# Numerators of batches 1 to 3 split at the halves of the tokens (288 and 256 columns) instead of 512 and 32

## The chip, the cores and the metric

The kernel runs on one core of one Trainium2 chip. The metric is the device time of one execution in microseconds. Before the change three runs took 291.69, 292.36 and 292.44 us: a median of 292.36 us.

The engines are named as in the profile: PE is TensorE (matmuls; PEld is its loading of weights), DVE is VectorE, ACT is ScalarE, POOL is GpSimd, SP is SyncE, which issues DMAs. Matmuls write to PSUM; DVE and ACT read PSUM and write SBUF.

## The reference

Two blocks, all in float32, with 4 batches, 4 heads, 1088 tokens in each, and head width 32.

```python
def phi(x):
    a = np.einsum('rd,bhsd->bhsr', S1, x)          # r = 8
    b = np.einsum('rd,bhsd->bhsr', S2, x)
    return np.einsum('bhsi,bhsj->bhsij', a, b).reshape(*x.shape[:-1], r * r)
q_p, k_p = (phi(q), phi(k))
kv = np.einsum('bhsf,bhsd->bhfd', k_p, v)
z = np.sum(k_p, axis=2)
num = np.einsum('bhsf,bhfd->bhsd', q_p, kv)
den = np.einsum('bhsf,bhf->bhs', q_p, z)[..., None] + 1e-06
attn = num / den
x = attn.transpose(0, 2, 1, 3).reshape(4352, 128)
gate = 1.0 / (1.0 + np.exp(-(x @ w_gate)))         # w_gate, w_val: 128 x 1536
return (gate * (x @ w_val)) @ w_out                # w_out: 1536 x 128
```

The change concerns `num`, the numerators, and their division by `den`.

## The kernel before, in words

**The second block sets the rhythm.** The tokens are cut into chunks of 512. For each chunk, twelve "waves" (function `w1`, matmuls of line 544) compute 128 columns each of both products with `w_gate` and `w_val` into a PSUM tile `wave` of two banks. There are two such buffers (pool `psm`). ACT takes the sigmoid (`sg`, line 552), DVE multiplies (`g`, function `glu` inside `w1`, line 587), POOL forms sums and differences of `g` (`tsum`, line 371), and further matmuls (`prod`, line 381) multiply by `w_out`. A wave may be written again only when DVE has read the wave that lay in its buffer.

**The first block is woven in between.** The order of the instructions on PE, DVE, ACT and POOL is written out by hand: each engine runs them in the order in which the code issues them. The function `slot(group, n)` issues a `group` of work of the first block and then `n` waves. Batch 0 is done at the start by functions of its own; batches 1 to 3 go through `begin`, `outer`, `sum_z`, `kv_all`, `ndt`, `qmult`, and last `parts`, at fixed places between the waves. So `parts` is called three times. The waves that read a batch's tokens come after its `parts`.

**The tokens of a batch stand in two halves.** `q_chk = [(0, 8), (8, 9)]` cuts the 34 rows of 32 tokens into pairs: 8 pairs and 9 pairs. Half 0 has 8 x 32 = 256 columns for each of two values of `c` (the two members of a pair), half 1 has 9 x 32 = 288 (`W1`). `QP[b]` holds the features `q_p` of both halves, and `half(t, n)` cuts half `n` out.

**What `parts(b)` does before** (lines 1267 to 1299):

1. `den_j` (line 1024): eight matmuls of 160 columns into the tile `denj` of the pool `ps2`, tag `two`, which has one buffer of two banks. Then DVE multiplies these 160 columns of each bank by `A8` into `PD` (line 1037). In the text this product is called `pd`.
2. `glu()`: DVE's product for the last wave.
3. Eight numerator matmuls (`numerators`, line 1259; one for each head and each `c`, 64 rows by 32 columns of the array, so that all eight run beside each other) with 512 columns: 256 of half 0 and the first 256 of half 1. They write a `wave` buffer, called `nps`.
4. ACT copies them to SBUF (`num`, line 1274, 128 x 1024), which lets the wave buffer go.
5. Eight numerator matmuls with the last 32 columns of half 1, in a new tile of tag `two` (`nps2`, in the profile also `nps`), columns 160 to 191. It is the buffer of `denj`, so the matmuls wait for `pd`.
6. `den_i` (line 1040): two matmuls of 160 columns that finish the denominators, in columns 0 to 159 of the same tile.
7. `turn_den` (line 1051): DVE transposes the denominators, adds 1e-6 and takes the reciprocal.
8. For each half: DVE spreads the reciprocals (`rb`, line 1282) and multiplies the numerators by them into `xT` (line 1293): 8 pairs of half 0 from `num`, 8 pairs of half 1 from `num`, and the ninth pair of half 1 from `nps2`.

After `parts`, `slot` issues the `prod` matmuls that are due and the next wave.

Of the kernel before, what the change touches and what calls it, by code (L numbers as in the profile page):

```python
# [8 lines left out]
F32 = mybir.dt.float32  # L9
# [5 lines left out]
MUL = ALU.mult  # L15

P = 128
# [3 lines left out]
def kernel(  # L21
# [12 lines left out]
    nc = tc.nc  # L34

    B, H, S, D = q.shape
# [24 lines left out]
    psm = ctx.enter_context(tc.tile_pool(name="psm", bufs=2, space=bass.MemoryType.PSUM))  # L61
    pso = ctx.enter_context(tc.tile_pool(name="pso", bufs=1, space=bass.MemoryType.PSUM))
    ps2 = ctx.enter_context(tc.tile_pool(name="ps2", bufs=1, space=bass.MemoryType.PSUM))
# [11 lines left out]
    q_chk = [(0, 8), (8, TP - 8)]  # L75
    T0 = 2 * q_chk[0][1]
    W1 = 32 * q_chk[1][1]
# [142 lines left out]
    def step(name, *parts, **how):  # L220
        for n in parts if wide else ():
            if n not in short:

                i = ((slice(0, 2), 0), (slice(0, 2), 1), (2, slice(0, 2)))[n] if n < 3 else (slice(0, 3), n - 1)
                pair, jj = (0, i[1]) if n < 3 else divmod(n - 1, 2)
                short[n] = Short(w_sb[:, i[0], i[1]], w_in[pair][:, i[0], jj])
            getattr(short[n], name)(**how)
# [92 lines left out]
    for c in range(2):  # L320
        rows = slice(64 * c, 64 * c + 64)
        nc.vector.tensor_reduce(
            out=m_col[rows, c],
            in_=ident[rows].rearrange("p (k j) -> p j k", j=R),
            axis=mybir.AxisListType.X,
            op=ALU.add,
        )
    for t, x in (
# [5 lines left out]
        out=e_sum,  # L334
        in_=bass.AP(
            tensor=e_row.tensor,
            offset=e_row.offset,
            ap=[list(e_row.ap[0]), [0, 2], [1, R], [0, R]],
        ),
# [3 lines left out]
    two = const.tile([P, 1], F32, tag="two_", name="two_")  # L343
# [5 lines left out]
    xT = const.tile([P, NTOK], F32, tag="xT")  # L349
# [258 lines left out]
    def glu():  # L608
        if moe["gate"] is not None:
            moe["gate"]()  # L610
            moe["gate"] = None
# [54 lines left out]
    KP, QP, BQ, ND, KAB, ASB, KVZ, KVD, Z4, ZS, A8, B8, ZW, PD, RC = ({} for _ in range(15))  # L666

    WD = 160
# [100 lines left out]
    def half(t, n):  # L769
        return t.rearrange("p (n h w) -> p n h w", n=2, h=H)[:, n, :, : 32 * q_chk[n][1]]  # L770
# [253 lines left out]
    def den_j(b):  # L1024
        t = ps2.tile([P, 2, 512], F32, tag="two", name="denj")
        for pi in range(2):
            rows = slice(64 * pi, 64 * pi + 64)
            for x in range(4):
                nc.tensor.matmul(  # L1029
                    out=t[32 * x : 32 * x + 32, pi, :WD],  # L1030
                    lhsT=ZW[b][rows, 4 * (x % 2) : 4 * (x % 2) + 4].rearrange("p x i -> p (x i)"),
                    rhs=B8[b][rows, (W1 - WD) * (x // 2) : (W1 - WD) * (x // 2) + WD],
                    start=True,
                    stop=True,
                )
        PD[b] = sbA.tile([P, 2, WD], F32, tag="pd", name="pd", bufs=1)
        nc.vector.tensor_tensor(out=PD[b], in0=t[:, :, :WD], in1=A8[b], op=MUL)


    def den_i(b, dps):  # L1040
        for pi in range(2):
            nc.tensor.matmul(  # L1042
                out=dps[64 * pi : 64 * pi + 64],
                lhsT=mask["head"].rearrange("p m x -> p (m x)"),
                rhs=PD[b][:, pi, :],
                start=True,
                stop=True,
            )
        return dps

    def turn_den(b, dps):
        nt, over = WD // 32, (W1 - WD) // 32
        dT = sbA.tile([P, nt, 32], F32, tag="dTi", name="dTi", bufs=1)
        nc.vector.transpose(out=dT.rearrange("p t c -> p (t c)"), in_=dps)
        RC[b] = sbA.tile([P, 2, W1 // 32, 2], F32, tag="rci", name="rci")
        for t0, t1, u0, k in ((0, nt, 0, 0), (nt, W1 // 32, nt - over, 4)):
            nc.vector.tensor_scalar_add(
                RC[b][:, :, t0:t1],
                dT[:, u0 : u0 + t1 - t0, k : k + 4].rearrange("p t (n c) -> p n t c", n=2),
                1e-6,  # L1060
            )
        nc.vector.reciprocal(out=RC[b], in_=RC[b])


    def dn(b, n, mid=None):
# [32 lines left out]


        def divide(*parts, between=None, later=False):  # L1100
            if mid is None:
                turn()
# [39 lines left out]
    else:  # L1142
        nc.vector.tensor_copy(
            out=s4[:, 1:],
            in_=bass.AP(
                tensor=s4.tensor, offset=s4.offset, ap=[list(s4.ap[0]), [0, 3], [1, D]]
            ),
# [5 lines left out]
        out=st_[:, : 2 * R],  # L1153
        lhsT=s4.rearrange("p g d -> p (g d)"),
        rhs=ident[: 2 * R, : 2 * R],
# [8 lines left out]
        out=sk,  # L1164
        in0=bass.AP(
            tensor=st_.tensor, offset=st_.offset, ap=[list(st_.ap[0]), [0, 2], [R, 2], [1, R]]
        ),
        in1=bass.AP(
            tensor=hm.tensor, offset=hm.offset, ap=[list(hm.ap[0]), [R, 2], [0, 2], [1, R]]
        ),  # L1170
        op=MUL,
# [6 lines left out]
    for n, inner in enumerate(([[1, R], [0, R]], [[0, R], [1, R]])):  # L1178
        t = const.tile([P, R, R], F32, tag=f"s{n}", name=f"s{n}")
        s0 = st_[:, n]  # L1180
        nc.scalar.copy(
            out=t, in_=bass.AP(tensor=s0.tensor, offset=s0.offset, ap=[list(s0.ap[0])] + inner)
# [68 lines left out]
        glu()  # L1251
        late.append(dn(0, 1)(later=True))

    def numerators(b, t, rest):
        for h in range(H):
            for c in range(2):
                rows = slice(64 * c, 64 * c + 64)
                q1 = QP[b].rearrange("p (n h w) -> p n h w", n=2, h=H)[rows, :, 2 * (h % 2) + h // 2]
                nc.tensor.matmul(  # L1259
                    out=t[32 * h : 32 * h + 32, c],  # L1260
                    lhsT=ND[b][rows, 32 * h : 32 * h + 32],
                    rhs=q1[:, 1, W1 - 32 :] if rest else q1[:, :, : W1 - 32],
                    start=True,
                    stop=True,
                )

    def parts(b):
        den_j(b)
        glu()
        t = psm.tile([P, 2, 512], F32, tag="wave", name="nps")  # L1270
        numerators(b, t, False)
        num = sbA.tile([P, 2, NJK, 2, F], F32, tag="kp", name="num", bufs=1)
        num = num.rearrange("p c j m f -> p (c j m f)")[:, :1024].rearrange("p (c w) -> p c w", c=2)
        nc.scalar.copy(out=num, in_=t)
        t = ps2.tile([P, 2, 512], F32, tag="two", name="nps2")
        numerators(b, t[:, :, WD : WD + 32], True)
        turn_den(b, den_i(b, t[:, 0, :WD]))
        for n in range(2):
            rb = sbA.tile([P, 9, 2, 32], F32, tag="rb", name="rb")
            t0, tn = q_chk[n]  # L1280
            r0 = RC[b][:, n]
            nc.vector.transpose(
                out=rb[:, :tn].rearrange("p t c s -> p (t c s)"),
                in_=bass.AP(
                    tensor=r0.tensor,
                    offset=r0.offset,
                    ap=[list(r0.ap[0]), [1, 2 * tn], [0, 32]],
                ),
            )
            for u0, u1, x in ((0, 8, num[:, :, 256 * n : 256 * n + 256]), (8, tn, t[:, :, WD : WD + 32])):  # L1290
                if u0 < u1:
                    o = b * S + 64 * (t0 + u0)
                    nc.vector.tensor_tensor(
                        out=xT[:, o : o + 64 * (u1 - u0)].rearrange("p (t c s) -> p c t s", c=2, s=32),
                        in0=x.rearrange("p c (t s) -> p c t s", s=32),
                        in1=rb[:, u0:u1].rearrange("p t c s -> p c t s"),
                        op=MUL,
                    )
        moe["ready"] = b * S + S

    def kv_all(b):
# [31 lines left out]
    load_kq(2)  # L1333
    slot(None, 1)
    slot(lambda: parts(1), 1)
    moe["store"]()

# [64 lines left out]
```

## Time and profile before

| what | value |
|---|---|
| three runs, median | 291.69, 292.44, 292.36; 292.36 us |
| the profiled execution | 291.03 us, of it the span from the first to the last instruction 289.2 us |
| granted TensorE clock, mean | 1.000 |
| numerators, 512 columns: 48 records, median | 589 ns |
| numerators, 32 columns: 48 records, median | 201 ns |
| pd, 128x320: 3, median | 492 ns |
| copy num, 128x1024: 3, median | 1012 ns |
| products from num, 128x512: 6, median | 693 ns |
| product from nps, 128x64: 3, median | 218 ns |

A matmul of float32 leaves two records in the trace, two passes over its columns. Records of matmuls that stand in different parts of the array overlap, and the length of a record includes the way through the array; so the time that a group of matmuls occupies the array is read from the distance of starts, not from the lengths. All times in the views are microseconds from the span's start, if not marked otherwise.

### The profile page before, as it was taken

The page shows a single profiled execution, that of the slowest core. Times are in us where ns is not written, and L with a number is a line of the kernel's source. Part 1 is how long each engine was busy: PE and PEld are TensorE (multiplying, and loading weights), DVE is VectorE, ACT ScalarE, POOL GpSimd, SP SyncE. Part 2 cuts the span into 40 slices and gives each one's busy share as a digit, 9 for nine tenths or more (in the row PEclk, how much of TensorE's full clock was granted, in tenths as well). Part 3 has the DMA queues.
Part 4 walks back from the last instruction along what each step waited for, and adds up shares of the span by engine and source line. Part 5 has one row for each costly group of instructions (what it writes and reads, how often), then busy time and mean ns, then how long its engine had stood idle before and what let it go on. Part 6 is the DMA issues. An engine that isn't in the chain of part 4 may idle for free.

```text
span 289.2 us, 5782 instructions
## 1 busy us (share of the span) xinstructions
PE 282.5 (98%) x2260; PEld 151.2 (52%) x2260; DVE 170.2 (59%) x294; ACT 106.5 (37%) x215; POOL 159.6 (55%) x222
## 2 busy tenths in 40 slices
PE   7799999999999999999999999999999999999995
PEld 3454433354444444444554445774555555555894
DVE  6977788945748547657556584737335223522471
ACT  3788732222334322523234222523243223422341
POOL 2666682667465387363465596563565646555200
PEclk9999999999999999999999999999999999999999
DMA  7995441765600396315001862020000100020011
GB/s 218 346 360 123 105 155 43 173 145 129 193 1 2 77 194 166 93 28 164 1 0 41 188 164 61 0 33 6 0 3 15 22 2 0 2 36 1 0 21 36
DMA packets 28890, 24.22 MB, mean 84 GB/s; under 512 B 18560, under 2 KB 24064, under 8 KB 28864
## 3 DMA queue, kind: packets, MB, share of 16 engines
q1 hardware_dynamic: 25888, 22.10, 29.9%
q10 hardware_dynamic: 2976, 1.77, 2.1%
q8 instruction: 17, 0.28, 0.4%
q14 instruction: 9, 0.07, 0.1%
HBM read 20.60 MB, written 3.26 MB: 82 GB/s over the span
## 4 chain that ended last, share of the span: by engine, by line
PE 95%; DVE 1%; DMA 1%; ACT 1%; issue 0%; POOL 0%; SPq 0%; DVEq 0%
PE wave L544 62%; PE prod L381 22%; PE moeout L425 4%; PE moeout L451 2%; PE kvz L900 1%; PE nps L1259 1%; PE kps L681 1%; DMA s_in<-in_S_dram 1%; PE cqps L827 1%; PE nps L1090 0%; PE denj L1029 0%; PE dps L1071 0%; PE nps L1042 0%; ACT asb L798 0%; DVE kT L650 0%
## 5 line engine op out<-in xcount | busy, mean ns | idle before, releaser
L544 PE MATMUL wave<-xT,w_sb 128*64 128x512 f32 (+3 forms) x820 | 210.2, 565 | 0.0
L552 ACT ACTIVATE sg<-wave 128x512 f32<-128x512 f32 x102 | 60.9, 597 | 159.6 <-PE wave L544 153.6
L587 DVE TENSOR_TENSOR g<-wave,sg 128x512 f32<-128x512 f32 x96 | 66.1, 688 | 91.0 <-ACT sg L552 88.0
L544 PEld LDWEIGHTS wave<-xT,w_sb 128*64 128x64 f32 (+1 forms) x820 | 84.0, 140 | 65.8 <-issue 49.4
L371 POOL TENSOR_TENSOR tsum<-g,tsum 128x256 f32<-128x256 f32 x84 | 69.4, 826 | 65.7 <-DVE g L587 65.7
L371 POOL TENSOR_TENSOR tsum<-g 128x256 f32<-128x256 f32 x84 | 65.2, 777 | 28.7 <-DVE g L587 28.0
L381 PE MATMUL prod<-tsum,ws 128*64 128x256 f32 x252 | 70.3, 380 | 0.0
L381 PE MATMUL prod<-g,w_sb 128*64 128x256 f32 x168 | 50.2, 380 | 0.0
L381 PEld LDWEIGHTS prod<-tsum,ws 128*64 128x64 f32 x252 | 32.9, 137 | 10.6 <-issue 7.3
L381 PEld LDWEIGHTS prod<-g,w_sb 128*64 128x64 f32 x168 | 22.7, 137 | 24.5 <-issue 20.6
L381 PE MATMUL prod<-tsum,w_sb 128*64 128x256 f32 x84 | 25.1, 381 | 0.0
L381 PE MATMUL prod<-g,ws 128*64 128x256 f32 x84 | 25.0, 379 | 0.0
L162 POOL TENSOR_TENSOR head<-head,tail 128x384 int32<-128x384 int32 (+1 forms) x13 | 13.2, 1022 | 4.4 <-DVE head L157 4.4
L381 PEld LDWEIGHTS prod<-g,ws 128*64 128x64 f32 x84 | 11.5, 137 | 4.1
L425 PE MATMUL moeout<-g,w_sb 128*128 128x512 f32 (+1 forms) x28 | 12.4, 599 | 0.0
L381 PEld LDWEIGHTS prod<-tsum,w_sb 128*64 128x64 f32 x84 | 10.5, 136 | 1.8 <-issue 1.0
L580 DVE TENSOR_TENSOR g<-wave,sg 128x512 f32<-128x512 f32 x6 | 6.7, 1116 | 6.4 <-ACT sg L552 6.4
L760 DVE TENSOR_TENSOR kp<-kab 128x1152 f32<-128x1152 f32 (+2 forms) x10 | 10.4, 1054 | 0.0
L880 DVE TENSOR_TENSOR qp<-qp,bq 128x1152 f32<-128x1152 f32 (+1 forms) x7 | 9.4, 1350 | 0.0
L141 POOL TENSOR_SCALAR head<-cap 128x384 f32<-128x384 f32 (+1 forms) x13 | 6.3, 488 | 5.0 <-ACT cap L140 5.0
L493 DVE TENSOR_TENSOR res<-prod,other 128x256 f32<-128x256 f32 x14 | 5.9, 423 | 4.7 <-ACT other L484 3.5
L425 PEld LDWEIGHTS moeout<-g,w_sb 128*128 128x128 f32 (+1 forms) x28 | 4.2, 174 | 6.2 <-issue 3.7
(130 smaller groups left out, 197.8 us busy)
## 6 DMA issues: line engine op xcount, KB each, us to landing
qp<-dq SPq DMA_DIRECT2D x7, 576.0 KB, 10.8
bq<-dq SPq DMA_DIRECT2D x14, 288.0 KB
kq<-in_k_dram SPq DMA_DIRECT2D x3, 544.0 KB
kq<-in_q_dram SPq DMA_DIRECT2D x3, 544.0 KB, 5.4
w_in<-in_moe_w_out_dram SPq DMA_DIRECT2D x6, 256.0 KB, 6.8
w_in<-in_moe_w_gate_dram SPq DMA_DIRECT2D x5, 256.0 KB
w_in<-in_moe_w_val_dram SPq DMA_DIRECT2D x5, 256.0 KB, 5.7
v<-in_v_dram SPq DMA_DIRECT2D x8, 144.0 KB
```

Of the source, the lines that this page charges most:

```text
L141: nc.gpsimd.tensor_scalar(out=self.head.bitcast(F32), in0=self.cap, scalar1=122880.0, scalar2=2.0**-15, op0=ALU.min, op1=ALU.max,)
L162: nc.gpsimd.tensor_tensor(out=self.head, in0=self.head, in1=self.tail.bitcast(I32), op=ALU.add)
L371: nc.gpsimd.tensor_tensor(out=t[:, u], in0=in0, in1=in1, op=ALU.subtract)
L381: nc.tensor.matmul(out=out, lhsT=lhsT, rhs=rhs, start=start, stop=stop, skip_group_check=True)
L425: nc.tensor.matmul(out=moe["acc"][d], lhsT=w_sb[:, 2, j, d], rhs=g[:, jj], start=(j == 0), stop=(j == NJ - 1),)
L493: nc.vector.tensor_tensor(out=out, in0=in0, in1=in1, op=ALU.add)
L544: nc.tensor.matmul(out=wv[d, which, jj * tw + o : jj * tw + o + tp], lhsT=w_sb[:, which, j0 + jj, d], rhs=xT[:, t0 + o : t0 + o + tp], sta ...
L552: nc.scalar.activation(out=sg, in_=wv[:, 0], func=ACTF.Sigmoid)
L580: nc.vector.tensor_tensor(out=g.rearrange("p (j u s y) -> p j y u s", j=2, u=2, y=4), in0=wv[:, 1].rearrange("p (j y u s) -> p j y u s", j ...
L587: nc.vector.tensor_tensor(out=g, in0=wv[:, 1], in1=sg, op=MUL)
L760: eng.tensor_tensor(out=KP[b][:, pi, j0:j1].rearrange("p j m (i l) -> p (j m) i l", i=R), in0=bass.AP(tensor=a0.tensor, offset=a0.offset, ...
L880: nc.vector.tensor_tensor(out=q0, in0=q0, in1=half(BQ[b], n), op=MUL)
```

## The change

`parts` now splits the numerators at the halves. Half 1 (288 columns) goes to a `wave` buffer first and is copied to SBUF by ACT (128 x 576). Half 0 (256 columns) goes to columns 160 to 415 of the tile `denj` itself, which `den_j` now returns, and DVE multiplies it straight out of PSUM. `den_i` writes columns 0 to 159 of that tile, as before. Each half has one product in place of one and two.

```diff
@@ den_j
         nc.vector.tensor_tensor(out=PD[b], in0=t[:, :, :WD], in1=A8[b], op=MUL)
+        return t
@@ numerators
-    def numerators(b, t, rest):
+    def numerators(b, n, t):
         for h in range(H):
             for c in range(2):
                 rows = slice(64 * c, 64 * c + 64)
-                q1 = QP[b].rearrange("p (n h w) -> p n h w", n=2, h=H)[rows, :, 2 * (h % 2) + h // 2]
                 nc.tensor.matmul(
                     out=t[32 * h : 32 * h + 32, c],
                     lhsT=ND[b][rows, 32 * h : 32 * h + 32],
-                    rhs=q1[:, 1, W1 - 32 :] if rest else q1[:, :, : W1 - 32],
+                    rhs=half(QP[b], n)[rows, 2 * (h % 2) + h // 2, :],
...
@@ parts
-        den_j(b)
+        t = den_j(b)
         glu()
-        t = psm.tile([P, 2, 512], F32, tag="wave", name="nps")
-        numerators(b, t, False)
+
+        (_, n0), (_, n1) = q_chk
+        x1 = psm.tile([P, 2, 512], F32, tag="wave", name="nps")[:, :, : 32 * n1]
+        numerators(b, 1, x1)
         num = sbA.tile([P, 2, NJK, 2, F], F32, tag="kp", name="num", bufs=1)
-        num = num.rearrange("p c j m f -> p (c j m f)")[:, :1024].rearrange("p (c w) -> p c w", c=2)
-        nc.scalar.copy(out=num, in_=t)
-        t = ps2.tile([P, 2, 512], F32, tag="two", name="nps2")
-        numerators(b, t[:, :, WD : WD + 32], True)
+        num = num.rearrange("p c j m f -> p (c j m f)")[:, : 64 * n1].rearrange("p (c w) -> p c w", c=2)
+        nc.scalar.copy(out=num, in_=x1)
+        x0 = t[:, :, WD : WD + 32 * n0]
+        numerators(b, 0, x0)
         turn_den(b, den_i(b, t[:, 0, :WD]))
-        for n in range(2):
+        for n, x in ((0, x0), (1, num)):
             rb = sbA.tile([P, 9, 2, 32], F32, tag="rb", name="rb")
...
-            for u0, u1, x in ((0, 8, num[:, :, 256 * n : 256 * n + 256]), (8, tn, t[:, :, WD : WD + 32])):
-                if u0 < u1:
-                    o = b * S + 64 * (t0 + u0)
-                    nc.vector.tensor_tensor(
-                        out=xT[:, o : o + 64 * (u1 - u0)].rearrange("p (t c s) -> p c t s", c=2, s=32),
-                        in0=x.rearrange("p c (t s) -> p c t s", s=32),
-                        in1=rb[:, u0:u1].rearrange("p t c s -> p c t s"),
-                        op=MUL,
-                    )
+            o = b * S + 64 * t0
+            nc.vector.tensor_tensor(
+                out=xT[:, o : o + 64 * tn].rearrange("p (t c s) -> p c t s", c=2, s=32),
+                in0=x.rearrange("p c (t s) -> p c t s", s=32),
+                in1=rb[:, :tn].rearrange("p t c s -> p c t s"),
+                op=MUL,
+            )
```

In the text x1 stands for the numerators of half 1 (288 columns) and x0 for those of half 0 (256 columns).

## The prediction

> **What bounds the kernel now.** I read the engine shares first, then the busy time by stretches, then who waited for whom on PE.
>
> ```profile
> PE 282.5 (98%) x2260; PEld 151.2 (52%) x2260; DVE 170.2 (59%) x294; ACT 106.5 (37%) x215; POOL 159.6 (55%) x222
> 72.00:131.00 59.00, 59.00 (x500) 27.07 (x498) 36.98 (x60) 20.16 (x40) 34.57 (x46) 1.00 0.41 96
> 131.00:196.00 65.00, 65.00 (x529) 36.13 (x528) 39.20 (x62) 21.25 (x42) 39.82 (x49) 1.00 0.28 71
> PE nps L1090 <- ACT nd L973: 0.4, 1, 0.4
> ```
>
> In the stretch rows the first figure after the colon is the stretch, the second PE's busy time: 59.00 of 59.00 us and 65.00 of 65.00, at a granted clock of 1.00 (the figure after the brackets). The last line is the latest of the six waits that the view of PE's waits lists; all six lie before 13.3 us. After that PE never waits for another engine. So what counts is PE's own time; work taken from DVE or ACT is worth nothing unless PE waits for it, and a gap newly put into PE is paid in full.
>
> The three calls of parts stand at 72.0, 131.4 and 196.1 us and look alike. This is the timeline of the first (start, length, engine):
>
> ```profile
> 72.04 0.50 PE L1029 MATMUL denj<-b,zw 64*32 64x160 f32 x16
> 72.34 1.16 PE L1259 MATMUL nps<-qp,nd 64*32 64x512 f32 x32
> 72.66 0.49 DVE L1037 TENSOR_TENSOR pd<-denj,a 128x320 f32<-128x320 f32 x1 [1.68 <-DMA v<-in_v_dram]
> 73.06 0.68 DVE L587 TENSOR_TENSOR g<-wave,sg 128x512 f32<-128x512 f32 x1
> 73.20 0.19 PEld L1259 LDWEIGHTS nps<-qp,nd 64*32 64x32 f32 x16 [0.70 <-DVE pd L1037]
> 73.43 0.49 PE L1042 MATMUL nps<-pd,head 128*64 128x160 f32 x4
> 73.52 1.01 ACT L1274 COPY num<-nps 128x1024 f32<-128x1024 f32 x1 [0.76 <-PE nps L1259]
> 73.75 0.38 PE L381 MATMUL prod<-g,w_sb 128*64 128x256 f32 x1
> ```
>
> The second line merges both numerator groups: 16 records of 512 columns (two per matmul) and 16 of 32. The weights of the 32-column group (73.20) are held by pd, DVE's product, since that group writes the buffer that pd reads. pd ends at 72.66 + 0.49 = 73.15; a waiter follows some 0.05 later (nd ends at 12.93 + 0.27 = 13.20 and the weights that wait for it start at 13.25). So the wait ends at 73.20. In narrower windows the second eight records of the 512 group start at 72.77, 0.43 after the first: its columns have streamed at 72.34 + 2 x 0.43 = 73.20. The two meet: the 0.70 is idle time of the weight loader alone, and the array covers it with the 512-column group.
>
> **The change part by part.** *PE.* Per call it issues the same 18 matmuls after denj; the numerators' columns are 8 x (512 + 32) before and 8 x (288 + 256) after, so their streaming is equal. What changes is where the wait for pd falls. In the built program the first 288-column matmul waits for DVE's count before pd (nothing new), and the first 256-column matmul for the count that pd raises, the same as the 32-column group waited for. I price the groups by rows of the same shape in batch 0:
>
> ```profile
> 13.25 0.67 PE L1090 MATMUL nps<-qp,nd 64*32 64x256 f32 x16 [0.36 <-ACT nd L973]
> 13.84 0.69 PE L827 MATMUL cqps<-qT,skq 64*32 64x288 f32 x8
> 46.37 0.72 PE L681 MATMUL kps<-kT,sk 64*32 64x288 f32 x16
> 46.88 0.69 PE L827 MATMUL cqps<-qT,skq 64*32 64x288 f32 x16
> ```
>
> Eight 288-column matmuls occupy the array for 46.88 - 46.37 = 0.51, so x1 is done at 72.34 + 0.51 = 72.85 at the latest (by 0.43 x 288/512 per pass at 72.82). denj and pd do not move, so x0 can load its weights only at 73.20: 0.35 us of idle array that the 512-column group used to fill. Then eight 256-column matmuls that begin after a wait take 13.84 - 13.25 = 0.59 until the next group starts; den_i starts at 73.20 + 0.59 = 73.79. Before, the 32-column group took 73.43 - 73.20 = 0.23. Hence +0.36 per call, and 3 x 0.36 = +1.09 us (0.364 before rounding). Both ends: x0's first matmul also waits for a DMA's count. The DMA is old, and one wait more cost 0.06 at the dps matmuls near 10.8 us (0.11 behind the DVE reduction instead of 0.05), so 0.42 per call at most, 1.27 in all. If the wait for pd fell away, x1 and x0 would follow each other: 72.34 + 0.48 + 0.43, 0.05 for the staggered starts and 0.09 for the change of tile shape before den_i make 73.39 instead of 73.43, -0.04 per call. I take +0.36: wait and durations each have a row.
>
> A rule speaks against hoping for that lower end. The Trainium skill (PSUM — Partial Sum Buffer, "PSUM bank collisions raise a hardware error") asks to guard PSUM by bank and quadrant, not by address. x0 sits in other columns of the banks that pd reads; by the rule the wait stays (+1.09), by addresses alone it could go (-0.12). The 0.70 row cannot tell the two apart, since the 32-column group was another tile in the same buffer.
>
> A rule speaks for the change: TensorE: Matmul & The Clock Gate ("Wait — 56ns, not 53.3ns?") gives matmuls a start-to-start floor of about 25 ns. Sixteen 32-column records would then cost 0.40 us, their removal would save that, and the call would lose 0.59 - 0.40 = 0.19, 0.57 in three. The row has all sixteen inside 0.23 us, 14 ns each at most, so the row decides.
>
> *ACT.* The copy of the numerators shrinks from 128x1024 (1.01) to 128x576; cq<-cqps of that shape takes 0.64. Nothing gained: PE did not wait for it, and its readers, the products at 76.00, had been able to read since 74.53.
>
> *DVE.* Two products instead of three. Before: 0.69 + 0.69 + 0.22 = 1.60. After: 256 columns per c from PSUM, between the L1109 rows of 0.425 (128x256) and 0.745 (128x576), by the slope 0.68; and 288 from SBUF, 0.693 x 576/512 = 0.78. Sum 1.46, -0.14. But DVE's chain hangs on den_i, so it starts 0.36 later and ends about 0.22 later. What is queued behind it:
>
> ```profile
> 78.02 0.22 DVE L1293 TENSOR_TENSOR xT<-nps,rb 128x64 f32<-128x64 f32 x1
> 78.16 0.68 DVE L587 TENSOR_TENSOR g<-wave,sg 128x512 f32<-128x512 f32 x1
> 79.13 0.36 PEld L544 LDWEIGHTS wave<-xT,w_sb 128*64 128x64 f32 x4
> ```
>
> g frees the wave buffer for the weights at 79.13: spare 79.13 - 78.84 = 0.29 before. After, g ends near 79.06 and the weights come at 79.49: spare 0.43. No new wait for PE, and POOL's sums, which read g, move with it. The g at 73.06 comes behind pd as before.
>
> *Buffers.* x0 keeps the buffer of denj until its product, near 77.1; the next writer is the kps of the next batch at 96.2. DMA issues and the queues of SP and POOL are untouched.
>
> Sum: 289.2 + 1.09 = 290.3 of span, with the 1.83 around it (291.03 - 289.2) 292.12 for the profiled execution. That one lay 1.33 below the median of the three runs; against the median the forecast is 292.36 + 1.09 = **293.45 us**.
>
> **The rivals.**
> 1. *Not slower: x0 does not wait for pd.* For it: pd reads columns 0 to 159, x0 writes from 160 on; den_i alone needs pd and could take the wait at the end of x0, 73.25, when pd is in. Against: the count in the built program. It decides if x0's weights load before pd's end. -0.12: 292.24. Chance 0.05.
> 2. *The delay is made good later.* If the waves after parts waited for DVE or POOL, PE's 0.36 would only eat that wait: 292.36. For it: DVE is behind there (sg of that wave ends at 76.55 + 0.60 = 77.15, its g starts at 78.16). Against: PE busy 59.00 of 59.00, no wait listed. Chance 0.11.
> 3. *DVE becomes the next wait as well.* If x0's product out of PSUM took the 1.12 of L580's permuted 128x512 form instead of 0.68, g would end at 79.50, the waiter follows 0.05 later, 79.55 against 79.49: 0.06 per call more; with the DMA wait's 0.06 too, 3 x 0.48 = 1.44 and 293.80. Against: L1109 has the very access pattern, at 0.745 for more columns. Chance 0.09.
>
> **How the numbers follow.** Forecast 0.75, rivals 0.05, 0.11, 0.09. The bounds of the PE term give 293.4 to 293.6, rival 3 reaches 293.8, and the three runs before spread by 0.75, so I add some 0.4 above. Below, the range goes toward rivals 1 and 2 far enough to leave out most of their 0.16 but not the noise of the forecast: 292.5 to 294.2. A measurement of this kernel can tell about 0.3%, 0.88 us, from no change; the forecast of 1.09 (0.37%) lies close above that. With a spread of about 0.3 on a difference of medians it is over 0.88 three times in four: slower 0.57 of its 0.75, plus rival 3's 0.09: 0.66. Faster can only come from rival 1 and chance: 0.04. Same: 0.30.
>
> **What would show it.** Right: in each call the 288-column records start where the 512 ones did, 0.30 after denj; the weights of the 256-column group start 0.05 after pd's end, with PE idle about 0.35 before them; den_i starts 1.75 us after denj's first matmul instead of 1.39; the wave 16 to 20 us further on is late by the same 0.36, and the second and third call by one and two times that. PE's waits gain pd with 3 entries and about 1.0 us. The copy takes 0.64, the products 0.68 and 0.78 with no third. Wrong: weights of the 256-column group loaded before pd ends (rival 1), the shift shrinking before the next call (rival 2), an idle PE before a wave with L587 as releaser (rival 3).

## The result and the profile after

| kernel | runs | median, us | lowest to highest | profiled execution | its span |
|---|---|---|---|---|---|
| before | 22 | 291.02 | 290.72 to 292.44 | 291.03 | 289.2 |
| after | 22 | 292.49 | 291.89 to 295.88 | 292.98 | 290.3 |

The changed kernel is slower: ratio 1.0055, interval [1.0036, 1.0074]. Lowest to lowest it is 291.89 - 290.72 = 1.17 us, in the spans of the two profiled executions 1.02 us (290.26 - 289.24). The difference of the medians, 1.47 us, holds more than that. Three of the 22 runs after (295.80 to 295.88 us), and one run of the kernel before on another chip (293.76 us), had a mean granted clock of 0.983 to 0.988 and took longest, so I do not count that to the change. And the time around the span, the run's time less its span, scatters: in the 22 runs after it lies between 1.74 and 2.68 us.

Where the time went is best read between two events that both kernels have: from the first matmul of the first wave (line 544) to the first matmul of line 451 near the end. Before, that is 276.94 - 14.50 = 262.44 us; after, 278.08 - 14.54 = 263.54 us (262.437 and 263.546 unrounded): +1.11. "The stretch" below means this. Its ends, in the kernel before and in the changed one:

```profile
14.50 1.78 PE L544 MATMUL wave<-xT,w_sb 128*128 128x256 f32 x7
276.94 1.09 PE L451 MATMUL moeout<-w_sb,g 128*64 128x128 f32 x16
```

```profile
14.54 1.78 PE L544 MATMUL wave<-xT,w_sb 128*128 128x256 f32 x7
278.08 0.99 PE L451 MATMUL moeout<-w_sb,g 128*64 128x128 f32 x14
```

First the busy time by windows after the change, PE's being the second figure after the colon, and the new entry in the list of PE's waits:

```profile
72.00:131.00 59.00, 58.83 (x499) 27.04 (x498) 37.21 (x59) 19.79 (x40) 34.15 (x46) 1.00 0.38 90
131.00:196.00 65.00, 64.83 (x529) 36.12 (x528) 39.46 (x61) 20.87 (x42) 39.52 (x48) 1.00 0.31 72
```

```profile
PE denj L1259 <- DVE pd L1037: 0.5, 3, 0.2
```

PE is no longer busy all the time: 0.17 us is missing in each window, and the list names the releaser, pd, three times (total us, times, longest). The clock is 1.00 as before. But 3 x 0.17 is 0.5, half of what was lost. Most of the other half is hidden by how a matmul is recorded. A record of a 288-column matmul lasts 0.40 us, though the group's second eight records start 0.24 us behind the first eight. So a record runs 0.16 us beyond the time that its columns keep the array, and a gap between the columns of two groups looks shorter by that. The timeline of the first call shows the gap by starts:

```profile
72.08 0.50 PE L1029 MATMUL denj<-b,zw 64*32 64x160 f32 x16
72.38 0.69 PE L1259 MATMUL nps<-qp,nd 64*32 64x288 f32 x16
72.69 0.49 DVE L1037 TENSOR_TENSOR pd<-denj,a 128x320 f32<-128x320 f32 x1 [1.68 <-PE denj L1029]
73.23 0.18 PEld L1259 LDWEIGHTS denj<-qp,nd 64*32 64x32 f32 x16 [0.70 <-DVE pd L1037]
73.24 0.67 PE L1259 MATMUL denj<-qp,nd 64*32 64x256 f32 x16 [0.17 <-DVE pd L1037]
73.83 0.49 PE L1043 MATMUL denj<-pd,head 128*64 128x160 f32 x4
```

The 288-column group starts at 72.38 and occupies the array for 0.51 (the distance of the rows at 46.37 and 46.88 before the change), to 72.89. pd ends at 72.69 + 0.49 = 73.18, the weights of the 256-column group follow 0.05 later at 73.23. So the array idles for 0.34 us, and den_i (line 1043) starts 73.83 - 72.08 = 1.75 us after denj instead of 1.39. The same 0.70 before the weights stood in the profile before too, but there the 512-column group filled it.

The calls inherit each other's delay in full. Start of denj in the three calls, and of line 451:

| | call 1 | call 2 | call 3 | L451 |
|---|---|---|---|---|
| before | 72.04 | 131.36 | 196.09 | 276.94 |
| after | 72.08 | 131.76 | 196.86 | 278.08 |
| later by | 0.04 | 0.40 | 0.78 | 1.15 |

The 0.04 is from the start-up ahead of the calls; the steps between are 0.37 us each (unrounded 0.367, 0.372 and 0.370).

On DVE the picture is less simple. These are DVE's groups after the change (total us, mean ns of one, then idle time before them), and behind them the one group before the change that they are to be set against:

```profile
L1293 DVE TENSOR_TENSOR xT<-num,rb 128x576 f32<-128x576 f32 x3 | 2.3, 758 | 0.3
L1293 DVE TENSOR_TENSOR xT<-denj,rb 128x512 f32<-128x512 f32 x3 | 2.1, 692 | 0.1
L1058 DVE TENSOR_SCALAR rci<-dTi 128x20 f32<-128x20 f32 x3 | 1.8, 615 | 0.1
```

```profile
L1057 DVE TENSOR_SCALAR rci<-dTi 128x20 f32<-128x20 f32 x3 | 0.9, 303 | 0.1
```

The products cost what was forecast, but the small addition of 1e-6, whose code the change does not touch, went from 303 to 615 ns. With that DVE's g of the next wave is late, and the weights that wait for its buffer come right behind it:

```profile
78.80 0.68 DVE L587 TENSOR_TENSOR g<-wave,sg 128x512 f32<-128x512 f32 x1
79.54 0.35 PEld L544 LDWEIGHTS wave<-xT,w_sb 128*64 128x64 f32 x4
```

g ends at 78.80 + 0.68 = 79.48 or 79.49; 0.05 for the waiter makes 79.54, the very start of the weights. So the distance from g's end to the weights, 0.29 us before, is down to the waiter's 0.05. PE still loses nothing by it, since these weights load 0.21 before their matmul (79.75).

### The profile page after: what moved, and what is told of

The parts are those of the page before. It is cut to its first block, busy times and chain, and to the rows that moved or that the text cites. A ratio compares the mean times of both kernels' runs of the same rounds, so it can differ in the third digit from the quotient of the medians.

```text
span 290.3 us, 5779 instructions
## 1 busy us (share of the span) xinstructions
PE 283.4 (98%) x2260; PEld 151.3 (52%) x2260; DVE 170.9 (59%) x291; ACT 105.4 (36%) x215; POOL 159.6 (55%) x222
## 4 chain that ended last, share of the span: by engine, by line
PE 95%; DVE 2%; DMA 1%; ACT 1%; issue 0%; POOL 0%; SPq 0%; DVEq 0%
PE wave L544 61%; PE prod L381 22%; PE moeout L425 4%; PE moeout L451 2%; PE kvz L900 1%; PE kps L681 1%; DMA s_in<-in_S_dram 1%; PE cqps L827 1%; PE denj L1259 1%; PE denj L1029 1%; DVE pd L1037 1%; PE nps L1091 0%; PE dps L1072 0%; PE denj L1043 0%; ACT asb L798 0%
```

## The experiments

One run tells the stretch closely (two profiles of the changed kernel gave 263.546 and 263.544 us), where medians need many runs. Most experiments are therefore single runs, read by their traces.

**The wait, made later and shorter.** In the first experiment the wave's `glu` goes ahead of pd, so that pd comes later and nothing else changes on PE:

```diff
@@ den_j
+        glu()
         PD[b] = sbA.tile([P, 2, WD], F32, tag="pd", name="pd", bufs=1)
         nc.vector.tensor_tensor(out=PD[b], in0=t[:, :, :WD], in1=A8[b], op=MUL)
@@ parts
         t = den_j(b)
-        glu()
```

> The changed kernel with pd put behind DVE's product g of the last wave instead of ahead of it; nothing else moves. The dose of the wait: g can start 0.05 after sg, 0.47 before pd's present end of start-up, and takes 0.68 with the next one starting 0.08 before its end; so pd ends 0.75 later. Theory: x0's weights follow 0.05 after pd's end, PE is idle 1.08 per call instead of 0.33, and nothing takes it back: +0.75 per call, span 290.3 + 2.25 = 292.55. Rival (later waits absorb what PE loses here): span below 291.5, with the shift shrinking between the calls.

In its timeline g now takes pd's place:

```profile
72.30 0.69 PE L1260 MATMUL nps<-qp,nd 64*32 64x288 f32 x16
...
73.37 0.48 DVE L1038 TENSOR_TENSOR pd<-denj,a 128x320 f32<-128x320 f32 x1
73.90 0.18 PEld L1260 LDWEIGHTS denj<-qp,nd 64*32 64x32 f32 x16 [1.45 <-DVE pd L1038]
```

The stretch is 265.74 us, 2.19 more than after, and the span 292.4 (one run: 294.41 us). The array idles for 1.09, 1.07 and 1.07 us in the three calls (73.90 - 72.30 - 0.51 in the first) instead of 0.34. Counted from denj, pd ends later than after the change by 0.74, 0.72 and 0.72 us, den_i starts later by the same, and these add up to the 2.19. So whatever pd is late by is paid in full, and nothing downstream makes it good.

The counterpart shortens pd: DVE multiplies only the first 32 of the 320 columns. `PD` is filled with ones ahead of time, so the denominators are other numbers.

```diff
@@ den_j (the filling of PD, earlier in the kernel, is left out here)
-        PD[b] = sbA.tile([P, 2, WD], F32, tag="pd", name="pd", bufs=1)
-        nc.vector.tensor_tensor(out=PD[b], in0=t[:, :, :WD], in1=A8[b], op=MUL)
+        nc.vector.tensor_tensor(out=PD[b][:, 0, :32], in0=t[:, 0, :32], in1=A8[b][:, 0, :32], op=MUL)
```

> The changed kernel with pd cut to the first 32 of its 320 columns; the rest of PD is set to 1 by POOL several waves earlier, so most denominators are left out. Order, shapes and waits on PE stay. pd should take about 0.19 instead of 0.49 (the 128x64 product took 0.22). Theory: x0's weights follow pd's end by 0.05 and so come 0.30 earlier; idle before x0 0.03 to 0.07 instead of 0.33. From the first wave's matmul to the first matmul of line 451: 263.55 after the change, 262.44 before; here 263.55 - 3 x 0.30 = 262.65 (262.6 to 262.8). Rival (the larger second group or its place in denj's banks costs by itself): 263.4 to 263.55.

Its timeline:

```profile
72.75 0.19 DVE L1038 TENSOR_TENSOR pd<-denj,a 128x32 f32<-128x32 f32 x1 [1.73 <-DMA v<-in_v_dram]
72.99 0.18 PEld L1260 LDWEIGHTS denj<-qp,nd 64*32 64x32 f32 x16 [0.46 <-DVE pd L1038]
...
73.59 0.49 PE L1044 MATMUL denj<-pd,head 128*64 128x160 f32 x4
```

pd takes 0.19, the weights start 0.05 behind it, and den_i starts 73.59 - 72.08 = 1.51 after denj. The idle time falls to 0.10 us (0.05 in the third call) and the stretch to 262.76, 0.79 less than after (span 289.5). It ends 0.1 above the expected middle and inside the expected bounds. Counted from denj, pd ends earlier by 0.24, 0.24 and 0.30 us, and den_i starts earlier by the same. With most of the wait gone, most of the loss is gone.

**The order of the groups.** If the loss is 0.05 behind pd plus all that stands behind the wait, it must grow with the columns put there. So half 0 goes first, into the wave buffer, and half 1 second:

```diff
-        x1 = psm.tile([P, 2, 512], F32, tag="wave", name="nps")[:, :, : 32 * n1]
-        numerators(b, 1, x1)
+        x0 = psm.tile([P, 2, 512], F32, tag="wave", name="nps")[:, :, : 32 * n0]
+        numerators(b, 0, x0)
...
-        x0 = t[:, :, WD : WD + 32 * n0]
-        numerators(b, 0, x0)
+        x1 = t[:, :, WD : WD + 32 * n1]
+        numerators(b, 1, x1)
... (the copy, now 128 x 512, and the products go with their halves)
```

> The changed kernel with the halves exchanged: x0 (256 columns) first, into the wave buffer and through ACT's copy; x1 (288 columns) second, in the tile denj. Theory: what counts is the columns that come after the wait for pd, whose end does not move: 32 columns more, 4 passes x 32 / 2.4 per ns = 0.05 per call, idle 0.38 instead of 0.33, span 290.3 + 0.16 = 290.45. Rival (the sum of the columns counts, or the copy's or the products' size): 290.3 or, by the shorter copy, less.

The stretch is 263.71, +0.16 against after (span 290.5). den_i starts at 74.00, 1.81 us after denj at 72.19, against 1.75: the wait ends where it did, and the 32 columns more behind it take 0.05 or 0.06.

Putting the 256 columns ahead of denj leaves nothing but den_i itself behind the wait:

```diff
-    def den_j(b):
+    def den_j(b, first):
         t = ps2.tile([P, 2, 512], F32, tag="two", name="denj")
+        first(t)
@@ parts
-        t = den_j(b)
+        t = den_j(b, lambda t: numerators(b, 0, t[:, :, WD : WD + 256]))
...
-        numerators(b, 0, x0)
```

> The changed kernel with one move: the eight 256-column matmuls of x0 go into the tile denj ahead of den_j's own matmuls, so pd is behind them and they wait for nothing. Shapes, buffers, copies and products stay as in the changed kernel. Theory (the cost is the array's idle time before x0, 0.33 us per call): no idle before x0; den_i now waits for pd instead. Per call from the first weights: 0.02 + 0.43 (x0) + 0.27 (denj), pd starts 1.04 after the first weights, ends at 1.53, den_i's weights at 1.58, against 1.75 in the changed kernel and 1.38 before. So -0.17 per call, span 290.3 - 0.5 = 289.8 (289.7 to 289.95). Rival (the two groups of 288 and 256 cost more by themselves than 512 and 32, for example because x0 lies in the banks of denj): the order changes nothing, 290.3.

Its timeline:

```profile
72.01 0.66 PE L1260 MATMUL denj<-qp,nd 64*32 64x256 f32 x16
72.47 0.48 PE L1030 MATMUL denj<-b,zw 64*32 64x160 f32 x16
72.74 0.69 PE L1260 MATMUL nps<-qp,nd 64*32 64x288 f32 x16
73.05 0.49 DVE L1038 TENSOR_TENSOR pd<-denj,a 128x320 f32<-128x320 f32 x1 [2.11 <-PE denj L1030]
73.60 0.49 PE L1044 MATMUL denj<-pd,head 128*64 128x160 f32 x4 [0.17 <-DVE pd L1038]
```

den_i waits for pd itself now, and starts 1.59 us after the call's first matmul, between before (1.39) and after (1.75). The stretch is 263.04, 0.50 less than after, as expected; the span 289.7. In seven runs the median was 292.68 us, ratio to before 1.0041 [1.0026, 1.0056]; this interval overlaps that of after, and only the trace tells the two apart. Still not as good as before: the 288 columns between denj and the wait do not cover pd in this order either, 512 did.

**A version that might beat both.** If the wait of 0.70 in the profile before had been lost time, then taking the 32-column group out of it ought to gain. So the kernel before gets its 32 columns ahead of denj, in the same tile (`den_j` is changed as in the last experiment and returns the tile):

```diff
@@ parts (of the kernel before)
-        den_j(b)
+        td = den_j(b, lambda t: numerators(b, t[:, :, WD : WD + 32], True))
...
-        t = ps2.tile([P, 2, 512], F32, tag="two", name="nps2")
-        numerators(b, t[:, :, WD : WD + 32], True)
+        t = td
```

> The kernel before with the same move: its eight 32-column matmuls go into the tile denj ahead of den_j's matmuls, then denj, then the 512-column group, then den_i. Theory: there was no idle time to win, since the 512-column group covered pd. The 32-column group needs 0.13 us less of its own group change but issues its 16 records in 0.11 ahead of denj: den_i's weights 1.39 after the first weights against 1.38, span 289.2 (289.05 to 289.35). Rival (the wait for pd listed at 0.70 per call was lost time already before the change): 0.2 to 0.7 per call come free, span 287.1 to 288.6.

It gains nothing, so the 0.70 was covered; but it loses, which I had not expected either: the stretch is 262.90, +0.46, and in 12 runs the median 291.80 us, ratio 1.0021 [1.0009, 1.0032]. The timeline, in which the 32-column group starts the call at 72.54:

```profile
72.54 0.18 PEld L1261 LDWEIGHTS denj<-qp,nd 64*32 64x32 f32 x16 [0.81 <-issue]
...
72.94 0.30 PEld L1261 LDWEIGHTS nps<-qp,nd 64*32 64x32 f32 x16
72.97 0.59 PE L1261 MATMUL nps<-qp,nd 64*32 64x512 f32 x1
...
74.08 0.49 PE L1044 MATMUL denj<-pd,head 128*64 128x160 f32 x4
```

den_i starts 1.54 after the call's first weights instead of 1.39. The weights of the 512-column group start 0.03 ahead of its first matmul (72.97); in the profile before it was 0.14 (72.20 to 72.34). It looks as if a group of 32 columns is over too soon for the next weights to load behind it, and that the delay is handed on; the 0.15 per call is measured, this cause is read from the rows and was not isolated.

**The DVE chain.** The prediction had DVE come out with more spare. To weigh it, the same DVE work (the spreading of the reciprocals of half 0 done once more) was added to each call in both kernels. It was expected at 0.65 us; in the first call it put off g by 0.71 us in both:

```diff
             for n, ... (both kernels, behind the products of half n)
+            nc.vector.transpose(
+                out=rb[:, :tn].rearrange("p t c s -> p (t c s)"),
+                in_=bass.AP(tensor=r0.tensor, offset=r0.offset, ap=[list(r0.ap[0]), [1, 2 * tn], [0, 32]]),
+            ) if n == 0 else None
```

> The kernel before with 0.65 us more for DVE in each call: the spread of the reciprocals of half 0 is done a second time, behind its use. The question is what DVE's time is worth to PE. g of the next wave would end at 79.49 instead of 78.84, and the weights that wait for it be loaded at 79.54 instead of 79.13; the matmul behind them started 0.21 after its weights. Theory (DVE's work is hidden up to the spare of some 0.29 to 0.5 us and costs only beyond it): 0.05 to 0.25 per call, so 262.6 to 263.2 from the first wave to line 451, against 262.44. Rival (DVE sets the pace behind parts): +0.65 per call, 264.4.

> The changed kernel with the same 0.65 us more for DVE in each call as in the run on the kernel before, where it cost 0.31 in the first call and nothing in the other two. The question is whether the change left DVE more spare (two products instead of three, 0.14 less) or less: in the changed trace the first small addition of turn_den takes 0.62 instead of 0.30, and g of the next wave ends 79.49, right at the load of the weights that wait for it (79.54; the matmul follows at 79.75). Theory (the longer addition ate more than the products gave): stall about 0.65 - 0.21 in the first call and 0.2 to 0.3 in the other two, so 264.3 to 264.8 from the first wave's matmul to the first matmul of line 451, against 263.55. Rival (the change left more spare, as the prediction had it): less than the 0.31 of the kernel before, 263.55 to 263.85.

In the first call of the kernel before and of the kernel after, each with the extra work, the weights of the wave wait:

```profile
79.72 0.20 PEld L544 LDWEIGHTS wave<-xT,w_sb 128*64 128x64 f32 x4 [0.55 <-DVE g L587]
```

```profile
80.32 0.20 PEld L544 LDWEIGHTS wave<-xT,w_sb 128*64 128x64 f32 x4 [0.79 <-DVE g L587]
```

On top of before the stretch grew by 0.47 us, of which 0.15 came ahead of any call and so not from the edit; in the calls it was 0.31, 0 and 0. On top of after it grew by 0.82: 0.56, 0.13 and 0.13. Both stretches, 262.90 and 264.37, lie inside their expected bounds, but not by the terms expected: the first call costs more than was said, the other two less. The change has left DVE less spare, not more. A smaller dose on the kernel before, the 64-column product done twice,

```diff
-                    nc.vector.tensor_tensor(
+                    for _ in range(2 if u0 else 1):
+                        nc.vector.tensor_tensor(
```

> The kernel before with the small product, 128x64, done twice in each call: 0.14 more for DVE, what the change takes away from it. Theory: inside the spare, so nothing: 262.44 (262.4 to 262.5) from the first wave to line 451. Rival (DVE sets the pace there, and the change's shorter DVE chain was worth something): +0.42 in three calls, 262.85.

moved g of the first call from 78.16 to 78.40 and the stretch by nothing: 262.44. The repeated product took 0.24 us and not the 0.14 expected. So before the change 0.24 us on DVE was free there.

**Why the addition doubled.** Each call makes two small additions, of 128x20 and 128x16, and the first seems to last until POOL's running sum ends. Before the change POOL's sum and the addition stood like this:

```profile
73.89 0.74 POOL L371 TENSOR_TENSOR tsum<-g,tsum 128x256 f32<-128x256 f32 x1 [1.19 <-DVE g L587]
74.35 0.38 DVE L1057 TENSOR_SCALAR rci<-dTi 128x20 f32<-128x20 f32 x2
```

and after it like this (the row of two holds the long and the short addition):

```profile
74.61 0.73 POOL L371 TENSOR_TENSOR tsum<-g 128x256 f32<-128x256 f32 x1
74.76 0.69 DVE L1058 TENSOR_SCALAR rci<-dTi 128x20 f32<-128x20 f32 x2
```

By single records the first addition ends at 74.657 before, 0.032 behind POOL's sum (74.625); at 75.377 after, again 0.032 behind it (75.345). In the third calls it is 0.034 and 0.032. The first addition's record starts 0.27 before the end of POOL's sum then, and 0.59 before it now: den_i is later by 0.37, and DVE's addition meets the next sum near its start instead of the last one near its end. The other experiments shift the addition against the sums too, and its length follows: 0.303 with pd late, 0.344 with the 32 columns first, 0.521 with x0 first, 0.557 with the halves exchanged, each time ending 0.03 behind the sum then running. The code of the addition is the same in all of them. The Trainium skill (SBUF — State Buffer, "Who interferes with whom") says that GpSimd and DVE share a pair of SBUF ports, that `tensor_scalar` can take the pair, and that whoever issues first holds it for the whole instruction while the other is blocked; by it a `tensor_tensor` with both inputs in SBUF is blocked by GpSimd's reads as well. That can be tried: the addition with a tile of constants as its second input.

```diff
-            nc.vector.tensor_scalar_add(
-                RC[b][:, :, t0:t1],
-                dT[:, u0 : u0 + t1 - t0, k : k + 4].rearrange("p t (n c) -> p n t c", n=2),
-                1e-6,
+            nc.vector.tensor_tensor(
+                out=RC[b][:, :, t0:t1],
+                in0=dT[:, u0 : u0 + t1 - t0, k : k + 4].rearrange("p t (n c) -> p n t c", n=2),
+                in1=...,  # eps, spread over p n t c
+                op=ALU.add,
             )
```

> The changed kernel with the two small additions of 1e-6 in turn_den done as DVE's two-input product form (an addition of a constant tile) instead of the form with an immediate. In all calls of both traces the first of them ends 0.03 after the end of the POOL sum that was running when it was issued (74.657 and 74.625 before, 75.377 and 75.345 after). Theory A (only the immediate form waits for POOL): the first addition takes 0.15 to 0.25, g of the next wave comes 0.3 to 0.45 earlier. Theory B (any addition with its inputs in SBUF waits for POOL): 0.5 to 0.7 as in the changed kernel. For PE neither matters: 263.5 to 263.6 from the first wave to line 451; the rival that DVE's chain sets PE's pace there would give 263.55 less 0.3 or more under theory A.

```profile
74.58 0.73 POOL L371 TENSOR_TENSOR tsum<-g 128x256 f32<-128x256 f32 x1
74.73 0.70 DVE L1058 TENSOR_TENSOR rci<-dTi,eps 128x20 f32<-128x20 f32 x2
```

The first addition still takes 0.615 us and ends at 75.343, 0.037 behind POOL's sum (75.306); the stretch is 263.55, as after. So the form with an immediate is not what makes it wait; the first additions agree with the skill's rule, in both of its forms. The other half of the rule, that POOL is blocked by DVE, does not show: the second addition of 0.161 us starts 0.01 before the next POOL sum, before the change and after it, and that sum still takes 0.737 us, where the median of all sums is 0.73. An addition that reads nothing by way of the shared ports was not tried, so the ports as the cause are argued; that the length is a wait for POOL's sum is shown.

**The changed kernel once more**, unedited, on another chip, for the size of the difference:

> The changed kernel once more, against the kernel before on one chip, to see what of the measured difference lies in the span. Theory: the stretch from the first wave's matmul to the first matmul of line 451 is 263.55 again against 262.44 (difference 1.11), and the spans differ by 0.9 to 1.2 in their medians; what the times differ by beyond that lies in the first 14.5 us and around the span and scatters. Rival (a second cost of the change, in a lower granted clock or after the span): the difference of the times stays 0.3 or more above that of the spans, or the clock is below 0.995 in several runs of the changed kernel and in none of the kernel before.

Twelve runs: median 292.37 us, 17 of the kernel before beside them 291.26; difference 1.11, ratio 1.0033 [1.0014, 1.0051]. The stretch of its profile is 263.54, as in the first profile of after. The medians of the spans are 290.3 and 289.5, 0.8 apart and a little under what was expected, with the spans before between 289.0 and 291.9. The times thus differ by 0.3 more than the spans, which is where the expectation put the bound of its rival. The granted clock is not it (0.996 or more in all twelve runs). The medians of the time around the span are not either (1.82 and 1.81 us), but its long tail is worth a look: it is above 2.2 us in 3 of these 12 runs and in 3 of the 22 above, but in 1 of 35 runs of the kernel before on two chips. The kernel before with its 32 columns first has it in 3 of 12 runs, so it does not come with the split; what brings it stays open.

## Why the prediction was right, and where it was not

*PE's term: right.* den_i 1.75 us after denj, as forecast; 0.34 us of idle array; 0.37 per call against 0.364; 1.11 in the stretch and 1.02 in the span against 1.09. The upper bound, a wait for an old DMA's count, did not come in: the weights follow pd's end by 0.05, not 0.11. That the loss is the wait, and nothing else in the change, is shown from both sides: pd later by 0.72 to 0.74 costs just that in each call, pd shorter gives back on average 0.26 per call of the 0.37 and leaves 0.10 of idle array. One account covers all orders tried: the end of the wait is set by denj (denj + 0.30 to start x1, pd's weights at denj + 1.15), and what stands behind the wait follows: 0.23 for 32 columns, 0.60 for 256, 0.65 for 288.

*Rival 1, x0 does not wait: fell.* Its weights load at 73.23, behind pd. The trace shows that the program waits; whether the chip would need the wait for other columns of the same bank was not tried.

*Rival 2, made good later: fell.* The delays stand at one, two and three times 0.37 at the next calls and at line 451, and even three times as large a delay was passed on whole.

*ACT and the products: right.* The copy takes 0.640 us; the products 0.692 and 0.758 against 0.68 and 0.78.

*DVE's chain: the step that was wrong.* "It starts 0.36 later and ends about 0.22 later", with the spare rising to 0.43. g came at 78.80 instead of 78.16; less the 0.04 of the start-up it is 0.60 later, and the distance from g's end to the weights shrank from 0.29 to 0.05 instead of growing to 0.43. The missing term is the addition's +0.31: 0.37 + 0.31 - 0.07 for the products with the gaps between them (forecast: -0.14) = 0.61. I had carried its 0.30 over from before as if it were the instruction's own length, when it was the rest of a POOL sum. Rival 3, DVE as the next wait, thus came within 0.2 us of deciding in the first call, by another mechanism than the slow product that it named; the 0.13 per call that after loses in calls two and three under the extra work, where before loses nothing, shows how near.

*PE's waits: half right.* Three entries of pd, but 0.5 us in place of about 1.0, since each record lasts 0.16 us beyond the time that its columns keep the array.

*The absolute time: the base was high.* 293.45 stood on three runs with a median of 292.36; 22 runs put the kernel before at 291.02. With 1.09 on top of that it is 292.11, against 292.49 measured. So the median stands at the very edge of the range, which had been drawn down to 292.5 for rivals 1 and 2 and not for a base that is too high. That the range reaches so far is luck; the difference of the stretches is not. The profiled execution took 292.98 against a sum of 292.12: its span of 290.3 was met, but the time around it was 2.7 us instead of 1.83.

## What to carry to other kernels

When two groups of matmuls lie around a wait, what counts is how many columns stand ahead of it and how many behind it, not their sum: put enough ahead to cover the producer, and as little as possible behind it. An idle time of the weight loader in a list of waits is a loss only if the array has run out of columns by then, so set the end of the columns (from starts) against the end of the wait. And before a small instruction's length is carried over to a new place, look whether it ends with an instruction of another engine: then it is a wait, and moving it changes it.

## What the runs showed of the hardware

- DVE's addition of 128x20 took 0.30 to 0.62 us depending on when it met a running POOL sum, and each time ended 0.03 to 0.04 behind that sum; with two inputs from SBUF it behaved the same.
- A 32-column group ahead of another group cost 0.15 us per call, though the call's columns were the same.
- Eight matmuls of 32 columns in different parts of the array, two records each, started 0.007 us apart (72.545 to 72.645 in the version with the 32 columns first).
